# Segment sums by accumulating DMAs on GpSimd's queue, with one short TensorE join, in an S5 convolution and memory-transformer kernel

## The chip, the cores and the metric

The kernel runs on one core of one Trainium2 chip. The metric is the device time of that core in microseconds (us), taken as the median over runs. The engines are named as in the profile: PE is TensorE (PEld its weight loads), DVE is VectorE, ACT is ScalarE, POOL is GpSimd, and SP is the engine that issues most of the DMAs.

## The reference, cut to what matters

Two results of 2048 x 1024 are put side by side. Part A is a state-space model; part B is a recurrent memory transformer over 64 segments of 32 rows, in which 8 memory rows pass from each segment to the next.

```python
def _B_ref(x, mem0, Wq, Wk, Wv, Wo, seg_len):       # x: 1 x 2048 x 1024
    mem = mem0                                       # 1 x 8 x 1024
    for s in range(n_seg):                           # 64 segments of 32 rows
        xs = x[:, s * seg_len:(s + 1) * seg_len, :].copy()
        h = jnp.concatenate([mem, xs], axis=1)
        q = jnp.einsum('btd,dhe->bhte', h, Wq)       # 32 heads of 128
        ...
        p = _softmax(scores, axis=-1)
        o = jnp.einsum('bhqk,bhke->bhqe', p, v)
        o = jnp.einsum('bhte,hed->btd', o, Wo)
        mem = o[:, :M, :].copy()
        outs.append(o[:, M:, :])
```

The kernel does not run the 64 segments one after another. It guesses the memory that each segment hands on, computes all segments at once, and compares the result with the guess at the end; only if they differ too much does a general loop run (it does not run here). The guess rests on the mean row of each segment: `xbar` is the sum of a segment's 32 rows of x, divided by 40 (segment 0 adds the 8 rows of mem0). The change concerns how these 64 sums, each 1024 wide, are formed.

## The kernel before, in words

The work falls into four stages on one program. Stage 1, to about 330 us of the span, is where the change lies. It alternates two kinds of steps that `steps()` lists in order:

- A step `v` (`v_x`) projects 512 rows of x by 512 columns of Wv: 32 matmuls into four PSUM banks `psP` (three buffers), which ACT copies to SBUF and writes out by DMA.
- A step `s` (`stage1`, numbered n = 0 to 31, eight groups `pc` of four blocks) is part A's input product and scan. PE makes 16 matmuls into `psU` (two buffers). DVE multiplies them by tables (`a_pr<-psU`), adds, and scans twice (`TENSOR_TENSOR_SCAN`). POOL then works out the start value of the next block from the scan's last column: five tiny instructions that end in `a_nx`, called the carry here, absent in the last block of each group. ACT copies the scans to `a_g`, DVE multiplies and adds again (`a_n`, `a_h`), and SP stores `a_h`.

A step s is followed by a step v, except after n = 6, 11, 16, 21, 26 and 30. In stage 1 the instructions of PE and of SP keep the order in which the program writes them (`k.pin`). On the other engines the scheduler may move an instruction ahead, unless it is marked `keep_in_program_order`.

The sums are made by the generator `sum_x`. It is first advanced at n = 1, where SP is given the loads of four tiles of 128 rows of x (`b_xr`, four buffers); then twice in each step from n = 3 on. Each advance takes one tile: eight matmuls with a 128 x 128 block of x as the stationary operand and the 128 x 4 indicator `k.ind` as the moving one, into a bank `psR`, and SP loads the tile that comes four later. So PE has 16 such matmuls ahead of the products of each of n = 3 to 10. At n = 11 the generator's last part lets DVE scale the bank into `xbar`. PE uses `xbar` first in `og`, after the v step behind n = 13.

`b_xr` first holds the four tiles from which the first v step gets its transposed x (`load_x0`, `turn_x0`), and last a block of zeros that `fill` writes to DRAM. `a.CT` is a tile in the pool `t32` that is loaded with part A's output weights from n = 17 on (`load_c`).

Of the kernel before, what the change touches and what calls it, by code (L numbers as in the profile page):

```python
# [8 lines left out]
FP32 = mybir.dt.float32  # L9
BF16 = mybir.dt.bfloat16  # L10
I32 = mybir.dt.int32
ACT = mybir.ActivationFunctionType
ALU = mybir.AluOpType
# [25 lines left out]
EV = E + 1  # L39
# [52 lines left out]
def consts(k):  # L92
    nc, V, G = k.nc, k.V, k.G
    c = k.cst
    k.ident = c.tile([128, 128], BF16, name="ident")
    G.memset(k.ident[:], 1.0)
    G.affine_select(out=k.ident[:], in_=k.ident[:], compare_op=ALU.is_equal, fill=0.0, base=0,
                    pattern=[[-1, 128]], channel_multiplier=1)
    k.ones = c.tile([128, 1], BF16, name="ones")
    V.memset(k.ones[:], 1.0)  # L100
    k.hpb = c.tile([128, 1], FP32, name="hpb")
    k.hpe = c.tile([128, 1], FP32, name="hpe")
    V.memset(k.hpb[:], HALF_PI)  # L103
    k.S.activation(k.hpe[:], k.hpb[:], ACT.Exp)
    k.ind = c.tile([128, 4], BF16, name="ind")
    G.memset(k.ind[:], 0.0)
    for j in range(4):
        G.memset(k.ind[32 * j:32 * j + 32, j:j + 1], 1.0)


def masks(k):
# [223 lines left out]
class PartB:  # L335
# [37 lines left out]

    def fill(self, tmp):
        k = self.k
        z = tmp.tile([32, 4 * EV], BF16, name="b_xr", bufs=4)
        k.V.memset(z[:], 0.0)
        for hb in range(HB):
            k.SP.dma_start(self.vx[hb][64 + NMX:GX, :], z[0:GX - 64 - NMX, :])
            k.SP.dma_start(self.vx[hb][T + 32:NSLOT, :], z[0:32, :])  # L380
        for q in range(4):
            k.SP.dma_start(self.tn[q][NM:NR, 0:4 * EV], z[0:NR - NM, :])
            k.SP.dma_start(self.tn[q][NM:NR, 1024 - 4 * EV:1024], z[0:NR - NM, :])
# [13 lines left out]
        return [(64 + 1536, 1536, 384), (0, XMAIN, 64), (T - 64, T - 64, 64)]  # L397

    def load_x0(self, tmp, i):
        self.x0.append(tmp.tile([128, D], BF16, name="b_xr", bufs=4))  # L400
        self.k.SP.dma_start(self.x0[i][:], self.x[0][64 + 128 * i:192 + 128 * i, :])

    def turn_x0(self, i):

        k = self.k
        pt = k.ps("U", (128, 2, KC, 128), BF16)[:, 0, :, :]
        for c in range(KC):
            k.PE.transpose(pt[:, c, :], self.x0[i][:, c * 128:(c + 1) * 128], k.ident[:])
        k.copy("vs"[i % 2], self.xe[:, :, 128 * i:128 * i + 128], pt)

    def sum_x(self, tmp):

        k = self.k
        xrs = {}

        def load(t):
            if t < TT:
                xrs[t] = tmp.tile([128, D], BF16, name="b_xr", bufs=4)
                k.SP.dma_start(xrs[t][:], self.x[0][t * 128:(t + 1) * 128, :])
        for t in range(4):  # L420
            load(t)
        yield
        p = k.ps("R")
        for t in range(TT):
            xr = xrs.pop(t)
            for c in range(KC):
                o = c * NSEG + 4 * t
                k.PE.matmul(p[:, o:o + 4], xr[:, c * 128:(c + 1) * 128], k.ind[:], start=True, stop=True)
            load(t + 4)
            yield  # L430
        pv = p[:].rearrange("p (c s) -> p c s", c=KC)
        ms = tmp.tile([128, KC], FP32, name="b_ms", bufs=1)
        k.V.tensor_reduce(ms[:], self.m0T[:], AX.X, ALU.add)
        k.V.tensor_scalar(self.xbar[:], pv, 1.0 / L, None, ALU.mult)
        k.V.tensor_tensor(ms[:], ms[:], pv[:, :, 0], ALU.add)
        k.V.tensor_scalar(self.xbar[:, :, 0], ms[:], 1.0 / L, None, ALU.mult)
        yield
# [483 lines left out]
def check_consts(k):  # L921

    V, G = k.V, k.G
    k.skip = k.cst.tile([128, 1], FP32, name="c_skip")
    G.memset(k.skip[:], 0.0)
    for r in (2, NTL - 2, NTL - 1):
        G.affine_select(out=k.skip[:], in_=k.skip[:], compare_op=ALU.not_equal, fill=1.0, base=-r,
                        pattern=[[0, 1]], channel_multiplier=1)
    k.fmask = k.cst.tile([L, 2, L], FP32, name="f_mask")
    G.memset(k.fmask[:], 1.0)  # L930
    G.affine_select(out=k.fmask[:, 0, :], in_=k.fmask[:, 0, :], compare_op=ALU.is_ge, fill=0.0, base=0,
                    pattern=[[-1, L]], channel_multiplier=1)
    G.memset(k.fmask[0:M, 0, :], 1.0)
    k.tc.keep_in_program_order(V.tensor_scalar(k.fmask[:, 1, :], k.fmask[:, 0, :], 1.0, 1.0e9, ALU.subtract, ALU.mult))


def steps():


    vs = [(pc, q) for pc in range(PC) for q in range(4)]  # L940
    vs[0:8] = [(i, q) for q in range(4) for i in range(2)]
    ss = [(pc, q) for pc in range(PC) for q in range(NB)]
    out = [("v",) + v for v in vs[:4]]
    vi = 4
    for n, s in enumerate(ss):
        out.append(("s",) + s)
        if n not in (6, 11, 16, 21, 26, 30) and vi < len(vs):
            out.append(("v",) + vs[vi])
            vi += 1
    return out + [("v",) + v for v in vs[vi:]]  # L950


def warm(k, pool):

    w = pool.tile([128, 512], BF16, name="a_n", bufs=1)
    k.V.memset(w[:], 0.0)  # L956
    p = k.ps("R")
    for _ in range(8):
        k.PE.matmul(p[:], w[:, 0:128], w[:], start=True, stop=True)
# [9 lines left out]
def kernel_main(tc, A_x, A_Lre, A_Lim, A_Bre, A_Bim, A_Cre, A_Cim, A_logdt, A_Dskip, B_x, B_mem0, B_Wq, B_Wk, B_Wv, B_Wo, out,  # L969
                force=False, dbg=None):  # L970
    with ExitStack() as ctx:
        k = K(tc, ctx)
        k.dbg = dbg
        nc = k.nc
        a = PartA(k, A_x, A_Lre, A_Lim, A_Bre, A_Bim, A_Cre, A_Cim, A_logdt, A_Dskip, out)
        b = PartB(k, B_x, B_mem0, B_Wq, B_Wk, B_Wv, B_Wo, out)

        def pool(name, side, bufs=2):
            return tc.tile_pool(name=name, bufs=bufs, side=side, reuse_waits="tile")
# [8 lines left out]
        with pool("p1x", "right") as p1x, pool("p1", "right", 1) as p1:  # L988
            a.tab = a.tmp = a.wp = a.btp = p1
            k.pin |= {"PE", "SP"}  # L990
            warm(k, p1)
            w0 = b.wl.tile([128, KC, 512], BF16, name="b_wv", bufs=2)
            b.load_wv_part(w0, 0, 0, 128, nc.scalar)
            b.x0 = []
            for i in range(4):
                b.load_x0(p1, i)
                if i in (1, 2):
                    b.load_wv_part(w0, 0, 128 * i, (256, 512)[i - 1])
            wv = {0: w0, 1: b.load_wv(1)}
            consts(k)  # L1000
            a.load_params(p1)
            b.load_m0(p1)
            b.stage_init()
            order = steps()
            b.v_x(0, 0, wv[0])
            b.load_x(1)
            a.load_b(0)
            a.xT = p1x.tile([128, KC, T], BF16, name="a_xT", bufs=1)
            a.load_x(0)
            a.params(p1, p1)  # L1010
            b.init(p1)
            a.tables(0)
            loads = [[(b, 2)], [(a, 1), (a, 2)], [(b, 3), (a, 3)]]
            sx = b.sum_x(p1)
            tabs = {0: a.tabs}
            bts = {0: a.bt}
            for kind, pc, q in order[1:]:
                if loads and kind == "v":
                    for o, n in loads.pop(0):
                        o.load_x(n)  # L1020
                if kind == "v":
                    b.v_x(pc, q, wv[pc])
                    if q == 3:
                        if pc >= 3:
                            b.og(pc, wv[pc])
                        n = (pc + 2) if pc + 2 < PC else (2, 0)[pc + 2 - PC]
                        wv[n] = b.load_wv(n)
                    continue
                a.tabs, a.bt = tabs[pc], bts[pc]
                n = 4 * pc + q  # L1030
                if q == 2 and pc + 1 < PC:
                    a.load_b(pc + 1)
                    bts[pc + 1], a.bt = a.bt, bts[pc]
                if pc >= 4 and q == 1:
                    a.load_c(pc - 4)
                if n == 1:
                    next(sx)
                if n >= 3:
                    for _ in range(2):
                        next(sx, None)  # L1040
                a.stage1(pc, q)
                if q == 2 and pc + 1 < PC:
                    a.tables(pc + 1)
                    tabs[pc + 1] = a.tabs
                if n == 12:
                    masks(k)
                    check_consts(k)
                if n == 14:
                    b.fill(p1)
            k.pin.remove("PE")  # L1050
# [7 lines left out]
        with pool("p2h", "right") as p2h, pool("p2", "right") as p2:  # L1058
# [5 lines left out]
            for i, _ in enumerate(s2):  # L1064
                if i in (1, 4, 7):
                    n = (2, 0, 1)[(i - 1) // 3]
# [148 lines left out]
```

## Time and profile before

| | |
|---|---|
| median of 8 runs | 1249.43 us (1249.01 to 1250.44) |
| the profiled execution's own time | 1249.28 us |
| its span in the profile | 1247.6 us |
| granted TensorE clock | 0.999 |
| PE busy | 1240.7 us, 99% |
| DVE, ACT, POOL busy | 667.8, 263.7, 273.3 us |
| matmuls of the sums (`psR<-ind,b_xr`) | 128 |
| DMA issues of the sums' tiles, on SP | 16 of 256 KB |

The span counts from the first to the last profiled instruction; 1.7 us of the execution's own time lie around it. In the profile a group's busy time is the union of its instructions, so that matmuls which overlap in the array's pipeline are not counted twice; the step from one matmul's start to the next is what one costs a full PE. A timeline row merges equal neighbours: start, length, engine, line, operation, tiles, count, and in brackets the idle time before it and what ended that.

### The profile page before, as it was taken

The numbers are of one execution on the slowest core, as the hardware profiler recorded it, in microseconds if no ns is written. First come the engines' busy times: TensorE is split into PE (matmuls) and PEld (weight loads), VectorE is DVE, ScalarE is ACT, GpSimd is POOL, SyncE is SP. The second block draws the span as 40 slices with busy tenths as digits, with TensorE's granted clock in tenths as the row PEclk, the third lists the DMA queues.
The fourth block names the chain that finished last, engine by engine and source line by source line (L and its number), as shares of the span: only waits on it lengthen the run. The fifth ranks groups of instructions, "written<-read, shape, count | busy, mean of one in ns | idle before, by whom it ended". The sixth has DMA issues, their size and how long they took to land.

```text
span 1247.6 us, 20183 instructions
## 1 busy us (share of the span) xinstructions
PE 1240.7 (99%) x8342; PEld 664.3 (53%) x8342; DVE 667.8 (54%) x1246; ACT 263.7 (21%) x631; POOL 273.3 (22%) x407
## 2 busy tenths in 40 slices
PE   9999999999999999999999999999999999999998
PEld 5444444444455555566666656555665554446444
DVE  4688899998711124666666666666666641001000
ACT  5344444443310000121212111111211110000000
POOL 3111331212332321222222222222222320000000
PEclk9999999999999999999999999999999999999999
DMA  9975444553898839334464544545474279407000
GB/s 239 243 220 145 128 135 125 141 152 107 238 319 248 249 113 248 91 88 121 90 146 106 142 106 113 140 90 131 93 160 93 56 225 206 108 18 153 18 17 27
DMA packets 314744, 174.18 MB, mean 140 GB/s; under 512 B 138648, under 2 KB 300048, under 8 KB 314648
## 3 DMA queue, kind: packets, MB, share of 16 engines
q1 hardware_dynamic: 292552, 146.22, 48.4%
q10 hardware_dynamic: 21072, 23.47, 5.9%
q0 software_dynamic: 1024, 3.17, 0.7%
q8 instruction: 66, 1.08, 0.4%
q14 instruction: 30, 0.25, 0.1%
HBM read 87.47 MB, written 52.19 MB: 112 GB/s over the span
## 4 chain that ended last, share of the span: by engine, by line
PE 99%; POOL 0%; ACT 0%; issue 0%; DVE 0%; ACTq 0%
PE psP L62 82%; PE psU L62 9%; PE psS L62 3%; PE psO L62 2%; PE psR L62 2%; POOL b_m L639 0%; ACT b_e L636 0%; DVE b_ost L89 0%; DVE a_n L956 0%; ACTq L87 0%; ACTq L636 0%; DVE hpb L103 0%; DVE ones L100 0%
## 5 line engine op out<-in xcount | busy, mean ns | idle before, releaser
L62 PE MATMUL psP<-b_xe,b_wq 128*128 128x480 bf16 (+1 forms) x1280 | 247.7, 342 | 0.0
L62 PE MATMUL psP<-b_xe,b_wk 128*128 128x480 bf16 (+1 forms) x1280 | 247.7, 343 | 0.0
L62 PE MATMUL psP<-b_wv,b_xe 128*128 128x512 bf16 (+2 forms) x1048 | 224.6, 373 | 0.0
L639 POOL TENSOR_TENSOR b_m<-b_e,maskB 99x396 bf16<-99x396 bf16 x160 | 139.4, 871 | 336.0 <-ACT b_e L636 336.0
L636 ACT ACTIVATE b_e<-psS 99x396 bf16<-99x396 f32 x176 | 88.0, 500 | 534.5 <-PE psS L62 526.9
L62 PEld LDWEIGHTS <-b_wk 128*128 128x128 bf16 x1280 | 119.3, 98 | 94.5
L62 PEld LDWEIGHTS <-b_wq 128*128 128x128 bf16 x1280 | 118.5, 98 | 88.1
L62 PEld LDWEIGHTS <-b_xe 128*128 128x128 bf16 x1056 | 102.1, 98 | 118.9 <-DVE b_xe L89 0.2
L89 DVE CAST b_k<-psP 128x480 bf16<-128x480 f32 (+1 forms) x192 | 98.1, 532 | 100.4 <-PE psP L62 100.4
L89 DVE CAST b_q<-psP 128x480 bf16<-128x480 f32 (+1 forms) x192 | 98.1, 532 | 93.8 <-PE psP L62 92.0
L62 PEld LDWEIGHTS <-b_ol 128*128 128x128 bf16 x864 | 84.3, 98 | 94.4
L62 PE MATMUL psU<-a_xT,a_bt 128*128 128x512 bf16 x512 | 114.9, 379 | 0.0
L62 PE MATMUL psP<-t,a_hl 128*128 128x512 bf16 x512 | 113.1, 379 | 0.0
L89 DVE CAST b_ost<-psP 128x512 bf16<-128x512 f32 (+1 forms) x17 | 11.5, 676 | 183.4 <-PE psP L62 183.4
L62 PE MATMUL psP<-wo,b_ol 128*128 128x512 bf16 (+1 forms) x448 | 92.5, 364 | 0.0
L62 PE MATMUL psP<-t,b_ol 128*128 128x512 bf16 x416 | 92.2, 379 | 0.0
L278 POOL TENSOR_SCALAR a_tt<-a_pr,a_tabf 128x1 f32<-128x1 f32 x48 | 34.0, 709 | 243.7 <-DVE a_pr L273 243.7
L87 ACT ACTIVATE b_vst<-psP 128x512 bf16<-128x512 f32 x126 | 72.4, 591 | 69.1 <-PE psP L62 60.2
L656 DVE TENSOR_TENSOR b_ob<-psO,b_accR 99x384 bf16<-99x384 f32 x160 | 85.9, 553 | 2.2
L265 DVE TENSOR_TENSOR a_pr<-psU,a_tabf 128x2048 f32<-128x2048 f32 x32 | 73.0, 2282 | 16.2 <-PE psU L62 16.1
L62 PEld LDWEIGHTS <-a_bt 128*128 128x128 bf16 x512 | 49.2, 98 | 57.6
L62 PEld LDWEIGHTS <-a_hl 128*128 128x128 bf16 x512 | 49.0, 98 | 56.7
(198 smaller groups left out, 964.6 us busy)
## 6 DMA issues: line engine op xcount, KB each, us to landing
b_v<-b_vx SPq DMA_DIRECT2D x16, 1064.2 KB
b_wv<-in_B_Wv_dram SPq DMA_DIRECT2D x16, 1024.0 KB
b_on<-b_ob SPq DMA_DIRECT2D x15, 960.0 KB
b_vx<-b_vst ACTq DMA_DIRECT2D x24, 516.0 KB
a_hs<-a_h SPq DMA_DIRECT2D x32, 256.0 KB
b_wog<-in_B_Wo_dram SPq DMA_DIRECT2D x4, 2048.0 KB
b_wq<-in_B_Wq_dram SPq DMA_DIRECT2D x16, 512.0 KB
b_wk<-in_B_Wk_dram SPq DMA_DIRECT2D x16, 512.0 KB
```

The source lines that it names most:

```text
L62: r = f(*a, **kw)
L87: self.S.activation(out, in_, ACT.Copy)
L89: self.V.tensor_copy(out, in_)
L265: V.tensor_tensor(pr[:], u[:].unsqueeze(1).to_broadcast([128, 2, 2, TB]), view(t3, [[TB + 1, 2], [TB + 1, 2], [1, TB]]), ALU.mult)
L278: G.tensor_scalar(tt[:, j:j + 1], w[:, j, TB - 1:TB], t3[:, 1, TB:TB + 1], None, ALU.mult)
L636: k.S.activation(e[:], s[0:GW], ACT.Exp, scale=float(E) ** -0.5, accum_out=self.accE[0:GW, i:i + 1])
L639: k.G.tensor_tensor(m[:, 0:4 * GW].rearrange("p (a b q) -> p a b q", a=2, b=2), e[:], mask[0:GW, :, :].unsqueeze(2).to_broadcast([GW, 2, 2 ...
L656: V.tensor_tensor(self.ob[:, b0:b0 + n, :], o[0:GW, 0:n, 0:E], r.unsqueeze(2).to_broadcast([GW, n, E]), ALU.mult)
```

## The change

`sum_x` no longer loads x in tiles of 128 rows. It views x as 128 half segments of 16 rows: partition p of the accumulator takes rows 16p to 16p + 15. Sixteen DMAs on GpSimd's queue each bring row j of all 128 half segments: the even j to one half of a float32 tile `acc`, the odd j to the other. The first DMA of each half writes, the other seven add to what is there. Two DMAs are issued per advance of the generator. Then POOL adds the two halves, ACT copies the sum to bf16 (the high part), and POOL subtracts the high part from the sum and stores the rest as bf16 (the low part); both lie in a corner of `a.CT`, which is not loaded yet. PE joins the half segments: 16 matmuls with a 128 x 128 block of the high or low part as the stationary operand, and a 128 x 64 indicator as the moving one, which has a one where partition p belongs to segment p // 2.

The generator is advanced once per step from n = 2 on. So the DMAs are issued ahead of n = 2 to 9, the three elementwise instructions ahead of n = 10, and the matmuls with DVE's scaling ahead of n = 11. The DMAs and POOL's two elementwise instructions are marked `keep_in_program_order`; ACT's copy is not. The indicator is built by one memset and two selections instead of five memsets, the four start tiles of `load_x0` become one tile of four parts, and all uses of `b_xr` now share a single buffer.

```diff
-    k.ind = c.tile([128, 4], BF16, name="ind")
-    G.memset(k.ind[:], 0.0)
-    for j in range(4):
-        G.memset(k.ind[32 * j:32 * j + 32, j:j + 1], 1.0)
+    k.ind = c.tile([128, NSEG], BF16, name="ind")
+    G.memset(k.ind[:], 1.0)
+    for base, m in ((0, 1), (1, -1)):
+        G.affine_select(out=k.ind[:], in_=k.ind[:], compare_op=ALU.is_ge, fill=0.0, base=base,
+                        pattern=[[-2 * m, NSEG]], channel_multiplier=m)
...
-        z = tmp.tile([32, 4 * EV], BF16, name="b_xr", bufs=4)
+        z = tmp.tile([32, 4 * EV], BF16, name="b_xr", bufs=1)
...
-        self.x0.append(tmp.tile([128, D], BF16, name="b_xr", bufs=4))
-        self.k.SP.dma_start(self.x0[i][:], self.x[0][64 + 128 * i:192 + 128 * i, :])
+        if i == 0:
+            self.x0 = tmp.tile([128, 4, D], BF16, name="b_xr", bufs=1)
+        self.k.SP.dma_start(self.x0[:, i, :], self.x[0][64 + 128 * i:192 + 128 * i, :])
...
-    def sum_x(self, tmp):
-
-        k = self.k
-        xrs = {}
-
-        def load(t):
-            if t < TT:
-                xrs[t] = tmp.tile([128, D], BF16, name="b_xr", bufs=4)
-                k.SP.dma_start(xrs[t][:], self.x[0][t * 128:(t + 1) * 128, :])
-        for t in range(4):
-            load(t)
+    def sum_x(self, tmp, ct):
+
+
+        k = self.k; G = k.G
+        acc = tmp.tile([128, 2, D], FP32, name="b_xr", bufs=1)
+        rows = self.x[0].rearrange("(p j) d -> p j d", j=16)
+        for j in range(16):
+            op = {"accum_op": ALU.add} if j > 1 else {}
+            k.tc.keep_in_program_order(G.dma_start(acc[:, j % 2, :], rows[:, j, :], **op))
+            if j % 2:
+                yield
+        s = acc[:, 0, :]
+        hl = ct[:, 0, 0:2, :]
+        k.tc.keep_in_program_order(G.tensor_tensor(s, s, acc[:, 1, :], ALU.add))
+        k.S.activation(hl[:, 0, :], s, ACT.Copy)
+        k.tc.keep_in_program_order(G.tensor_tensor(hl[:, 1, :], s, hl[:, 0, :], ALU.subtract))
         yield
         p = k.ps("R")
-        for t in range(TT):
-            xr = xrs.pop(t)
-            for c in range(KC):
-                o = c * NSEG + 4 * t
-                k.PE.matmul(p[:, o:o + 4], xr[:, c * 128:(c + 1) * 128], k.ind[:], start=True, stop=True)
-            load(t + 4)
-            yield
+        for c in range(KC):
+            for i in range(2):
+                k.PE.matmul(p[:, c * NSEG:(c + 1) * NSEG], hl[:, i, c * 128:(c + 1) * 128], k.ind[:], start=(i == 0), stop=(i == 1))
...
-                if n == 1:
-                    next(sx)
-                if n >= 3:
-                    for _ in range(2):
-                        next(sx, None)
+                if n >= 2:
+                    next(sx, None)
                 a.stage1(pc, q)
```

More of the change, by code (lines that the diff above doesn't have):

```diff
@@ L407, in turn_x0 @@
         for c in range(KC):
-            k.PE.transpose(pt[:, c, :], self.x0[i][:, c * 128:(c + 1) * 128], k.ident[:])
+            k.PE.transpose(pt[:, c, :], self.x0[:, i, c * 128:(c + 1) * 128], k.ident[:])
         k.copy("vs"[i % 2], self.xe[:, :, 128 * i:128 * i + 128], pt)
-    def sum_x(self, tmp):
-        k = self.k
-        xrs = {}
-        def load(t):
-            if t < TT:
-                xrs[t] = tmp.tile([128, D], BF16, name="b_xr", bufs=4)
-                k.SP.dma_start(xrs[t][:], self.x[0][t * 128:(t + 1) * 128, :])
-        for t in range(4):
-            load(t)
+    def sum_x(self, tmp, ct):
[12 more added lines that the diff above has]
+        k.tc.keep_in_program_order(G.tensor_tensor(hl[:, 1, :], s, hl[:, 0, :], ALU.subtract))
         yield
         p = k.ps("R")
-        for t in range(TT):
-            xr = xrs.pop(t)
-            for c in range(KC):
-                o = c * NSEG + 4 * t
-                k.PE.matmul(p[:, o:o + 4], xr[:, c * 128:(c + 1) * 128], k.ind[:], start=True, stop=True)
-            load(t + 4)
-            yield
+        for c in range(KC):
+            for i in range(2):
+                k.PE.matmul(p[:, c * NSEG:(c + 1) * NSEG], hl[:, i, c * 128:(c + 1) * 128], k.ind[:], start=(i == 0), stop=(i == 1))
         pv = p[:].rearrange("p (c s) -> p c s", c=KC)
@@ L993, in kernel_main @@
             b.load_wv_part(w0, 0, 0, 128, nc.scalar)
-            b.x0 = []
             for i in range(4):
@@ L1013, in kernel_main @@
             loads = [[(b, 2)], [(a, 1), (a, 2)], [(b, 3), (a, 3)]]
-            sx = b.sum_x(p1)
+            sx = b.sum_x(p1, a.CT)
             tabs = {0: a.tabs}
```

## The prediction

> **What bounds the kernel now.** I read the busy line and the chain of the page first, then PE's timeline around the sums, then DVE's and POOL's where the new instructions will stand, and last the DMA issues of POOL's queue.
>
> ```profile
> PE 1240.7 (99%) x8342; PEld 664.3 (53%) x8342; DVE 667.8 (54%) x1246; ACT 263.7 (21%) x631; POOL 273.3 (22%) x407
> PE 99%; POOL 0%; ACT 0%; issue 0%; DVE 0%; ACTq 0%
> ```
>
> PE is the path from end to end: the chain that ended last lies on it for 99%. Whatever PE no longer executes comes off the time, and whatever PE newly waits for goes on it, one for one. What the sums cost PE is seen in its timeline, at n = 6 and 7 of the steps s, and what 64-column matmuls cost, in `og`:
>
> ```profile
> 99.22 0.54 PE L62 MATMUL psR<-ind,b_xr 128*128 128x4 bf16 x16
> 99.62 3.61 PE L62 MATMUL psU<-a_xT,a_bt 128*128 128x512 bf16 x16
> 103.07 0.54 PE L62 MATMUL psR<-ind,b_xr 128*128 128x4 bf16 x16
> ...
> 170.28 1.10 PE L62 MATMUL psR<-b_xbar,b_wv 128*128 128x64 bf16 x32
> 171.22 2.11 PE L62 MATMUL psU<-a_xT,a_bt 128*128 128x512 bf16 x9
> ```
>
> Start to start, 16 sum matmuls hold PE for 0.40 us (25 ns each), not the 0.54 of the merged row, whose end overlaps the next group. The 32 of `og` hold it 0.94 us: 29 ns each.
>
> **What goes and what comes on PE.** Removed: 8 groups x 0.40 = 3.2 us. Added: 16 matmuls x 29 ns = 0.47 us. If nothing new makes PE wait, the gain is 2.73 us. The profiled execution (1249.28, span 1247.6) would read 1246.55; I set it against the median, 0.15 higher: 1249.43 - 2.73 = 1246.7.
>
> **Edits that I cost at nothing.** SP loses 16 issues of about 0.42 us; only the tile loads hung on them. The indicator, the joined start tile and the single `b_xr` buffer act at the start or at `fill`: `b_xr` is free from the last transposition (11.2 us) until the first accumulating DMA (after 58 us), and PE reads the identity, not the indicator, at the start. If the parts of the joined start tile were awaited together, PE would lose about 2 us there (the fourth load is issued at 3.3, the second at 1.3); separate parts of one tile are already awaited separately for Wv's first block, so I take zero. DVE's scaling of `psR` (1.0 us) stays, one step later; its reader `og` comes 24 us behind.
>
> **POOL's queue: what the DMAs pass.** Besides the carries POOL is idle in stage 1. Each DMA pair stands behind the carry of n - 1 and ahead of that of n, and waits for the landing of the pair before. Behind a waiting DMA stands a carry; for it waits DVE's scan of n + 1, and for DVE, through `psU`, PE.
>
> ```profile
> a_xn<-in_A_x_dram POOLq DMA_DIRECT2D x3, 256.0 KB, 6.2
> ...
> a_r<-in_A_Lambda_re_dram POOLq DMA_DIRECT2D x1, 2.0 KB, 4.2
> ...
> 330.36 2.23 POOL L306 DMA_DIRECT2D a_hl<-a_hs  x4 [0.41 <-issue]
> ```
>
> An issue costs POOL 0.56 us, so a pair 1.1 us. No row shows an accumulating DMA. Its time to landing is at least the 4.2 us of a 2 KB row. The nearest row is `a_xn`, plain and of the same source bytes: 6.2. Above that: a row now reads 2 KB and 4 KB and writes 4 KB, 10 KB for `a_xn`'s 4, so its 2.0 us over the small DMA become 5: 9.2 us. I take 7. The chain has room for that: steps are 10.4 us apart (without the sums), and where two steps s adjoin or a carry is absent there is a spare step. DVE has cover too: from the end of `a_pr<-psU` to PE's return to that bank are 5.5 us at worst (n = 20) and 7.9 or more at n = 2 to 13. A carry late by up to 4 us is absorbed.
>
> [...]
>
> **The join: the new wait on PE's own path.** PE comes to the joining matmuls at 146.11 - 3.2 = 142.9 us, behind the step v after n = 10, in fixed order: all of PE is queued behind them. Their input is a chain of last DMA pair, add, copy, subtraction.
>
> ```profile
> 130.06 0.20 POOL L280 TENSOR_TENSOR a_nx<-a_nx,a_tt 128x2 f32<-128x2 f32 x1
> 136.77 1.05 POOL L280 TENSOR_TENSOR a_nx<-a_nx,a_tt 128x2 f32<-128x2 f32 x1
> ...
> 136.54 1.23 DVE L284 TENSOR_TENSOR a_n<-a_g,a_tabh 128x2048 bf16<-128x2048 bf16 x1 [0.70 <-ACT a_g L274]
> 137.80 0.69 DVE L285 TENSOR_TENSOR a_h<-a_n 128x1024 bf16<-128x1024 bf16 x1
> 141.73 1.22 DVE L268 TENSOR_TENSOR a_pr<-a_pr 128x1024 f32<-128x1024 f32 x1
> 143.06 2.46 DVE L273 TENSOR_TENSOR_SCAN a_pr<-a_rr,a_nx,a_pr 128x512 f32<-128x512 f32 x2
> ```
>
> These instructions come 1.6 us earlier after the change (DVE is held by PE last at n = 6, with four groups gone). So the carry of n = 8 ends at 130.26 - 1.6 = 128.7, the last pair is issued to 129.8 and lands 7 us after its second start (129.2): 136.2. The carry of n = 9 ends at 137.82 - 1.6 = 136.2. Then the add, priced by POOL's row of this width, `a_xd` 128x1024: 2.12 us; behind DVE's `a_h` it runs 136.8 to 138.9. ACT's copy is 1.02 us by the `b_xe<-psU` row of 128x1024: to 140.1. The subtraction, 2.12 us again, ends at 142.3 to 142.5: 0.4 us ahead of PE.
>
> [...] In the rows above the same 128x2 instruction takes 0.20 us, and 1.05 us when it starts inside `a_n`, ending 0.05 us after it. [...] By the rows alone only POOL waits: if the subtraction misses the gap at 140.4 it starts behind the first scan (141.7) or the second (142.9), ends at 143.9 or 145.1, and PE waits 1.0 or 2.2 us. [...] I take the gap as met.
>
> ACT is idle in the window (before: 137.5 to 141.1, with the PE-fed copies to come 3.2 us earlier, at 137.9 and 139.6), so the copy fits between two of them, if it is ordered there. It is not pinned. Behind it in ACT's queue stand the `psP` copies, whose three buffers cover PE for 5.2 us.
>
> **The rivals.**
>
> *In time (chance 0.40).* The join finds its input: 1246.7. For it: the chain above with every price from a row; against it: a margin of 0.4 us.
>
> *The join is late by some microseconds (0.30).* The copy is ordered behind a `psP` copy or behind the `a_g` copies of n = 10 (144.38 and 145.56 before, 142.8 after), or the subtraction falls behind the scans, or the last pair lands at 137 to 140. With the copy after the first `a_g` of n = 10 (143.4), it ends at 144.4, the subtraction at 146.6, and PE waits 3.7 us: 1250.4. With one missed gap PE waits 1.0: 1247.7. Middle: 2 us, 1248.7. For it: everything that can vary makes the chain longer, and a lost gap costs a whole DVE instruction. Waits from 0.23 to 5.2 us mean no measurable change.
>
> *The accumulating DMAs are slow (0.30).* If one takes about 10 us or more, each pair holds up the next: the one ahead of n = 7 starts at 109 and is followed back to back by that of n = 8. At 12 us they land at 121.5 and 134; the last pair is issued at 134, holds up the carry of n = 9, and lands at 146.5; add, copy and subtraction end about 153 (2.1 + 1.1 + 2.1 + 1.2 for a lock), and PE waits 10.4 us: 1249.4 - 2.7 + 10.4 = 1257. It decides from about 10 us per DMA: there the last lands at 140.5, the chain ends near 148, and the wait of 5.2 us turns the gain into a loss of over 0.2%. For it: no trace row has this kind, DMAs are 0.62 busy at 128 to 140 us[...]. Against it: 10 us is beyond my upper bound of 9.2.
>
> *The change does not do what it says:* PE might keep its time if the loads, not the matmuls, paced these steps. It does not: PE has no idle time between 31 and 480 us.
>
> **How the numbers follow.** What a measurement of this kernel can tell from no change is about 0.2%, 2.5 us. Cases: 0.40 in time (faster: 2.73 is just over), 0.30 late by some microseconds (same), 0.30 slow DMAs (slower). Forecast: the likeliest, 1246.7. Low end 1246.2: no wait, and 0.5 us for the sizes of the two matmul rows. High end 1259: it takes in the slow case to 12 us per DMA with 2 us of lock and order on top; beyond lies a longer chain, about 1 in 8. The likeliest case alone: 1246.2 to 1247.2.
>
> **What would show it.** Right: 112 fewer matmuls; steps s at n = 3 to 10 10.36 us apart where they were 10.76; PE without idle time ahead of `psR<-ind,t`; POOL rows of 0.5 to 0.6 us for 16 DMAs, and landings near 7 us. Wrong: a wait of PE on `psR` for POOL's subtraction or for the DMA behind it (how late, read at its start against 142.9); POOL's carries waiting for a DMA; DVE instructions longer beside the add or the subtraction; PE waiting on `psU`, which I exclude.

## The result, and the profile after

The changed kernel takes 1254.48 us in the median of 21 runs (1252.96 to 1263.6), the kernel before, on the same chip, 1249.65. The ratio is 1.0042, 95% interval 1.0033 to 1.005: slower by about 0.4%, where 1246.7 and a gain had been forecast. The profiled execution took 1256.14 us, its span is 1254.3.

The first two lines are the page's busy line and its chain of the changed kernel.

```profile
PE 1239.4 (99%) x8230; PEld 661.0 (53%) x8230; DVE 667.9 (53%) x1246; ACT 264.4 (21%) x632; POOL 292.3 (23%) x423
PE 92%; DVE 3%; DMA 2%; POOL 1%; ACT 1%; issue 0%; SPq 0%; ACTq 0%; DVEq 0%; POOLq 0%
```

PE has the 112 matmuls fewer. Yet the chain that lay on PE for 99% does so for 92%: on the rest of it PE waits for others. The timeline of PE in the changed kernel, around the steps n = 9 to 13, shows where (start, length, instruction, count, idle time before it and what ended that):

```profile
124.89 3.62 PE L62 MATMUL psU<-a_xT,a_bt 128*128 128x512 bf16 x16
128.34 7.07 PE L62 MATMUL psP<-b_wv,b_xe 128*128 128x512 bf16 x32
135.25 3.62 PE L62 MATMUL psU<-a_xT,a_bt 128*128 128x512 bf16 x16
138.70 3.62 PE L62 MATMUL psP<-b_wv,b_xe 128*128 128x512 bf16 x16
145.55 3.61 PE L62 MATMUL psP<-b_wv,b_xe 128*128 128x512 bf16 x16 [3.23 <-ACT b_vst L87]
149.00 0.63 PE L62 MATMUL psR<-ind,t 128*128 128x64 bf16 x16
149.47 7.07 PE L62 MATMUL psU<-a_xT,a_bt 128*128 128x512 bf16 x32
156.37 5.34 PE L62 MATMUL psP<-b_wv,b_xe 128*128 128x512 bf16 x24
164.23 3.43 PE L62 MATMUL psP<-b_wv,b_xe 128*128 128x512 bf16 x8 [2.52 <-ACT b_vst L87]
```

The steps are 10.36 us apart now (135.25 - 124.89), and the sixteen joining matmuls take 0.47 us start to start (149.47 - 149.00). But the step v after n = 10 stops in its middle and the one after n = 12 after three quarters, both times for ACT's copies of `psP`. (Idle times in the text are taken from start to start, less the 0.216 us of a matmul, or the 0.03 us of one of 64 columns: 3.39 and 2.68 us here; the bracket counts from a modelled end.) The joining matmuls themselves wait for nothing.

**The first stop** is explained by ACT's timeline:

```profile
137.43 0.58 ACT L87 ACTIVATE b_vst<-psP 128x512 bf16<-128x512 f32 x1
143.95 1.06 ACT L427 ACTIVATE t<-b_xr 128x1024 bf16<-128x1024 f32 x1 [5.94 <-POOL b_xr L426]
144.92 0.58 ACT L87 ACTIVATE b_vst<-psP 128x512 bf16<-128x512 f32 x1
```

The copy of the sum's high part stands in ACT's queue ahead of the last `psP` copy of the previous step v. It waits 5.94 us for POOL's add, and everything behind it waits along. POOL's own timeline says why the add is late: the last two DMAs are issued from 131.28 on, and land 8.3 and 9.5 us after their issues began.

```profile
131.28 1.83 POOL L421 DMA_DIRECT2D b_xr<-in_B_x_dram  x2
...
141.58 2.34 POOL L426 TENSOR_TENSOR b_xr<-b_xr 128x1024 f32<-128x1024 f32 x1 [2.74 <-DMA b_xr<-in_B_x_dram]
145.09 2.12 POOL L428 TENSOR_TENSOR t<-b_xr,t 128x1024 bf16<-128x1024 f32 x1 [1.17 <-ACT t L427]
```

**The second stop** begins on DVE, one step of the pipeline earlier. First the changed kernel, then the same instruction in the kernel before:

```profile
147.32 0.27 DVE L378 MEMSET b_xr<- 32x258 uint32 x1 [7.81 <-POOL t L428]
147.52 2.22 DVE L266 TENSOR_TENSOR a_pr<-psU,a_tabf 128x2048 f32<-128x2048 f32 x1
```

```profile
129.01 0.27 DVE L377 MEMSET b_xr<- 32x258 uint32 x1
```

This is the memset of `fill`'s zeros. In the program it comes after n = 14; in both kernels it stands much earlier in DVE's queue. With four buffers nothing held it. With one, it needs the accumulator's buffer, which POOL's subtraction releases last, at 147.2. Behind it stands `a_pr<-psU` of n = 10. So DVE is 7.81 us idle and then late. PE does not wait for DVE through `psU` here; the delay reaches it through ACT, whose queue has the table work of the next group and the `a_g` copies ahead of the `psP` copies:

```profile
159.30 0.63 ACT L227 ACTIVATE a_tabf<-a_fr 128x513 f32<-128x513 f32 x1 [4.17 <-DVE a_pr L266]
...
163.06 0.63 ACT L275 ACTIVATE a_g<-a_pr 128x512 bf16<-128x512 f32 x1 [0.55 <-DVE a_pr L274]
163.60 0.58 ACT L87 ACTIVATE b_vst<-psP 128x512 bf16<-128x512 f32 x1
```

The table work waits for DVE's late `a_pr<-psU`; in the kernel before the same instruction starts at 152.15. The `psP` copy at 163.60 ends the stop of PE, two steps behind the memset.

The second stop costs more than its idle time. The windows of the changed kernel (length, then busy time and count of PE, PEld, DVE, ACT, POOL, then the granted clock, DMA share and GB/s):

```profile
161.00:164.20 3.20, 0.72 (x4) 0.20 (x3) 3.20 (x3) 2.44 (x6) 0.00 (x0) 1.00 0.00 0
164.20:167.50 3.30, 3.27 (x9) 1.20 (x9) 3.30 (x4) 1.56 (x3) 0.00 (x0) 0.53 0.00 0
167.50:171.00 3.50, 3.50 (x17) 1.58 (x16) 3.50 (x5) 1.74 (x3) 1.69 (x2) 0.95 0.19 75
```

The granted clock falls to 0.53: eight matmuls follow each other at 427 ns instead of 216, which adds 1.68 us. The page's clock row, in 40 slices, does not show this.

The spans divide as follows (first `psU` of n = 0; of n = 10; last of n = 31; end of DVE's last copy; end). The last column is the best kernel of the experiments, described below.

| stretch | before | after | best |
|---|---|---|---|
| start to n = 0 | 35.86 | 38.38 | 36.68 |
| n = 0 to n = 10 | 99.90 | 96.87 | 96.69 |
| n = 10 to n = 31 | 189.99 | 198.22 | 191.22 |
| n = 31 to the last copy | 917.53 | 917.55 | 917.54 |
| last copy to the end | 4.31 | 3.33 | 3.33 |
| span | 1247.59 | 1254.35 | 1245.47 |

The removed matmuls bring the second row down by 3.03 to 3.21. The third row of the changed kernel is +8.23 = 0.47 (joining matmuls) + 3.39 (first stop) + 2.68 + 1.68 (second stop, idle and half clock). The start of this execution is 2.5 later; in the other profiles with the new sums it is 0.6 to 1.0 later, except in one (2.6). The end is 0.98 shorter. With a start of 0.8 the rows sum to -3.0 + 8.2 + 0.8 - 1.0 = 5.0; the medians differ by 4.83.

### The profile page after: what moved, and what is told of

The parts are those of the page before. It is cut to its first block, busy times and chain, and to the rows that moved or that the text cites. A ratio compares the mean times of both kernels' runs of the same rounds, so it can differ in the third digit from the quotient of the medians.

```text
span 1254.3 us, 19944 instructions
## 1 busy us (share of the span) xinstructions
PE 1239.4 (99%) x8230; PEld 661.0 (53%) x8230; DVE 667.9 (53%) x1246; ACT 264.4 (21%) x632; POOL 292.3 (23%) x423
## 4 chain that ended last, share of the span: by engine, by line
PE 92%; DVE 3%; DMA 2%; POOL 1%; ACT 1%; issue 0%; SPq 0%; ACTq 0%; DVEq 0%; POOLq 0%
PE psP L62 78%; PE psU L62 7%; PE psS L62 3%; PE psO L62 2%; PE psR L62 1%; DVE a_pr L266 1%; DVE a_pr L274 1%; DMA b_xr<-in_B_x_dram 1%; DMA b_vx<-b_vst 1%; DMA b_wv<-in_B_Wv_dram 1%; DVE a_pr L269 0%; POOL b_m L642 0%; ACT b_vst L87 0%; DVE a_n L285 0%; POOL b_xr L426 0%
## 5 line engine op out<-in xcount | busy, mean ns | idle before, releaser
L62 PEld LDWEIGHTS <-b_xe 128*128 128x128 bf16 x1056 | 102.2, 98 | 128.6 <-issue 10.5
```

The lines of the kernel that those rows point to most:

```text
L62: r = f(*a, **kw)
```

## The experiments

The main theory, A in the expectations: two instructions that were moved ahead of their place hold their queues, ACT's copy and `fill`'s memset, and the sums themselves are not too dear. The rivals: the late join itself, and accumulating DMAs that are too slow. Each time is set against runs of the kernel before on the same chip.

**1. The zeros in a place of their own.** Only `fill` changes: the zeros take a spare corner of `a.CT`.

```diff
-        z = tmp.tile([32, 4 * EV], BF16, name="b_xr", bufs=1)
-        k.V.memset(z[:], 0.0)
+        z = ct[0:32, 0, 2, 0:4 * EV]
+        k.V.memset(z, 0.0)
```

> The changed kernel with the block of zeros of fill in a corner of a.CT instead of the single buffer b_xr; DVE's memset then goes first in its queue and waits for nothing. Theory A (two queues are held by the join: ACT's copy holds the psP copies, 3.4 us of PE at n = 10; DVE's memset holds a_pr, 4.2 us of PE at n = 12): the second stall goes, the first stays: 1249.65 - 2.73 + 3.4 = 1250.3, range 1249.6 to 1251.0. Theory B ([...] the memset only happens to stand there): DVE stays late, 1252.5 or more. Theory C (the accumulating DMAs slow other DMAs, PE's 2.5 us at the start and small stalls): no change, 1254.5.

Measured: 1251.31 us, ratio 1.0013 (1.0006 to 1.002). PE's timeline of this kernel:

```profile
137.21 3.62 PE L62 MATMUL psP<-b_wv,b_xe 128*128 128x512 bf16 x16
144.06 5.30 PE L62 MATMUL psP<-b_wv,b_xe 128*128 128x512 bf16 x16 [3.24 <-ACT b_vst L87]
...
156.57 7.07 PE L62 MATMUL psP<-b_wv,b_xe 128*128 128x512 bf16 x32
```

The second stop is gone: 32 matmuls in one row after n = 12. The first is there unchanged. So the shared buffer caused the second stop. The time is 0.3 above the expected band, and the row of 5.30 us where 3.61 stood tells why: now it is this stop that is followed by half clock (1.67 us).

**2. The copy on POOL** in place of ACT, in program order, with all else as changed.

```diff
-        k.S.activation(hl[:, 0, :], s, ACT.Copy)
+        k.tc.keep_in_program_order(G.tensor_copy(hl[:, 0, :], s))
```

> The changed kernel with the high part copied by POOL, pinned, instead of by ACT; ACT's queue no longer waits, the zeros still share b_xr. Theory A: the stall of 3.2 us in the step v after n = 10 goes, and PE waits about 1.5 us at the join for the subtraction instead; but DVE's memset still ends near 147.3 us, and as DVE's queue and not PE sets the stall at n = 12, that stall grows by what PE gained: 1254.5, range 1253.5 to 1255. If the two stalls simply add (rival to A): 1254.5 - 3.4 + 1.5 = 1252.6. Theory C: 1254.5, with both stalls still small beside the start.

Measured: 1255.72 us in the median of 5 runs, ratio 1.0044 (1.0031 to 1.0058): 0.7 above the expected band, and further from the rival's 1252.6. PE's timeline:

```profile
145.51 0.19 PE L62 MATMUL psR<-ind,t 128*128 128x64 bf16 x1
147.48 0.61 PE L62 MATMUL psR<-ind,t 128*128 128x64 bf16 x15 [1.77 <-POOL t L428]
...
164.44 2.66 PE L62 MATMUL psP<-b_wv,b_xe 128*128 128x512 bf16 x8 [4.26 <-ACT b_vst L87]
```

The first stop is gone, so ACT's copy caused it. Two things came in its place: PE now waits 1.94 us at the join itself, which the first stop had hidden, and the second stop grows from 2.68 to 4.42 us idle (half clock follows as before), because PE reaches it that much earlier while DVE is held as before. Both stops hang on the same late sum: with the copy mended alone, the second stop and the join take up the time. Not so the other way round: experiment 1 lost the second stop and kept the first at its length.

**3. Add and join one step later each**, by a `yield` more ahead of the add and one more ahead of the joining matmuls: the sum gets a whole step for its landing, and PE comes to the join at n = 13.

```diff
+        yield
         s = acc[:, 0, :]
...
         yield
+        yield
         p = k.ps("R")
```

> The changed kernel with an empty step behind the last DMAs and another ahead of the join: add, copy, subtraction ahead of n = 11, joining matmuls ahead of n = 13. The DMAs have landed by then. Theory A: ACT's copy stands where no step v follows at once, no stall from it; DVE's memset still waits for the subtraction, about 5 us instead of 7.8, and PE loses 1 us or less: 1248, range 1246.7 to 1249.5. Theory B: [...] 1249 or more. Theory C: 1252 or more, since the DMAs are all there.

Measured: 1251.42 us, ratio 1.0016 (1.0006 to 1.0025). The expectation was missed by about 3 us. ACT's copy still waits 3.15 us, but at a place where PE has cover. The memset is still on DVE's queue ahead of its place, waits 2.85 us, and PE stops once, with half clock after it:

```profile
150.58 5.34 PE L62 MATMUL psP<-b_wv,b_xe 128*128 128x512 bf16 x24
158.63 3.46 PE L62 MATMUL psP<-b_wv,b_xe 128*128 128x512 bf16 x8 [2.71 <-ACT b_vst L87]
```

I had taken the shorter wait on DVE as covered. It was not: idle 2.87 and 1.57 of half clock.

**4. Both: later, and the zeros apart** (the edits of experiments 1 and 3).

> Both edits, the later join and the zeros in a corner of a.CT. Theory A: no queue is held, what is left is the gain on PE: 1249.65 - 2.73 = 1246.9, range 1246.4 to 1247.7. Theory B: up to 2 us more. Theory C: 1252 or more. If the joined start tile costs PE about 1 us at the start, 1248.

Measured: 1247.75 us, ratio 0.9991 (0.9981 to 1.0). PE's timeline:

```profile
143.93 7.07 PE L62 MATMUL psU<-a_xT,a_bt 128*128 128x512 bf16 x32
150.84 7.31 PE L62 MATMUL psP<-b_wv,b_xe 128*128 128x512 bf16 x32
157.99 0.63 PE L62 MATMUL psR<-ind,t 128*128 128x64 bf16 x16
```

No stop of over 0.5 us is left in stage 1 (0.25 here, 0.49 at 202 us); the sums and the accumulating DMAs are as in the changed kernel. So the loss came from the late sum and the two queues that were held for it, and not from the DMAs' rate, which is the same here.

**5. The join at its own place with no queue held** (the edits of experiments 1 and 2): what the late join costs by itself.

> The changed kernel at its own place (join ahead of n = 11) with the zeros in a corner of a.CT and the copy on POOL: neither ACT's nor DVE's queue is held. What is left is PE's own wait at the join for the last DMAs, add, copy and subtraction, 2.0 us as in the kernel with the copy on POOL alone. 1249.5 - 2.73 + 2.0 = 1248.7; with 0.8 us at the start, 1249.5. If [...] PE waits at psU or psP as well, 1250.5 or more.

Measured: 1252.79 us, ratio 1.0026 (1.0015 to 1.0037): a time of the last case, 1250.5 or more, but not by the way named there, since PE waits at the join alone. First PE's timeline, then POOL's, then DVE's:

```profile
145.44 0.20 PE L62 MATMUL psR<-ind,t 128*128 128x64 bf16 x1 [1.36 <-POOL t L427]
148.43 0.61 PE L62 MATMUL psR<-ind,t 128*128 128x64 bf16 x15 [2.79 <-POOL t L428]
```

```profile
140.09 3.38 POOL L426 TENSOR_TENSOR b_xr<-b_xr 128x1024 f32<-128x1024 f32 x1 [2.96 <-DMA b_xr<-in_B_x_dram]
143.54 1.84 POOL L427 CAST t<-b_xr 128x1024 bf16<-128x1024 f32 x1
145.46 2.91 POOL L428 TENSOR_TENSOR t<-b_xr,t 128x1024 bf16<-128x1024 f32 x1
```

```profile
140.04 1.23 DVE L269 TENSOR_TENSOR a_pr<-a_pr 128x1024 f32<-128x1024 f32 x1
141.37 5.09 DVE L274 TENSOR_TENSOR_SCAN a_pr<-a_rr,a_nx,a_pr 128x512 f32<-128x512 f32 x2
147.16 2.30 DVE L285 TENSOR_TENSOR a_n<-a_g,a_tabh 128x2048 bf16<-128x2048 bf16 x1 [0.70 <-ACT a_g L275]
```

PE waits 1.52 and 2.96 us at the join, 4.48 in all where 2.0 were expected, and 1.69 of half clock follow. So a late join is enough to turn the gain into a loss, with no queue held. The chain is longer here than in the changed kernel. POOL's and DVE's instructions run side by side, and both take longer: the add takes 3.38 (2.34 above), the cast 1.84 (1.04 in experiment 2, where DVE stood still), the subtraction 2.91 (2.12), while the two scans take 5.09 (2.46) and `a_n` 2.30 (1.23). That is 0.79 to 1.04 us more for each of POOL's, 2.63 for the two scans together and 1.07 for `a_n`; by what means they lengthen each other is not shown. In the changed kernel itself it cost nothing, since DVE was idle at that time (7.81 us): with the queues mended, this loss comes to light.

**6. Later, zeros apart and the copy on POOL** (the edits of experiments 1, 2 and 3).

> Join two steps later, zeros apart, copy on POOL: no queue held, no wait at the join. Pure gain on PE: 1246.8; if the 0.8 us at the start of all changed kernels belong to the change, 1247.5. Range 1246.4 to 1247.8.

Measured: 1248.22 us, ratio 0.9996 (0.9987 to 1.0006), 0.4 above the expected range. PE's two waits are 0.61 and 0.50 us. With a step of time in between, no difference between ACT's copy (experiment 4) and POOL's is clear of the noise.

**7. What adding costs a DMA.** Experiment 1 with all sixteen DMAs overwriting, so that the rows are not summed, and the general loop left out.

```diff
-            op = {"accum_op": ALU.add} if j > 1 else {}
+            op = {}
```

> The 16 DMAs overwrite instead of adding (the rows are no longer summed), the check of the guess is set to pass, and the zeros are apart; same issues, same order, same waits. If the accumulation makes the late landing (9.6 us for the second DMA of the last pair), this one lands within 7.5 us and the stall of the copies shrinks by 2 us, to 1.5. If it is the issue on POOL and the queue that take the time, 9 us or more and the stall stays at 3.4.

Measured: 1248.14 us in one run. The rows of POOL's group and of the DMA issues, first of the changed kernel, then of this one:

```profile
L421 POOL DMA_DIRECT2D b_xr<-in_B_x_dram x16 | 13.8, 952 | 13.0 <-DMA b_xr<-in_B_x_dram 13.0
b_xr<-in_B_x_dram POOLq DMA_DIRECT2D x16, 512.0 KB, 7.5
```

```profile
L421 POOL DMA_DIRECT2D b_xr<-in_B_x_dram x16 | 9.0, 565 | 9.8 <-DMA b_xr<-in_B_x_dram 9.7
b_xr<-in_B_x_dram POOLq DMA_DIRECT2D x16, 512.0 KB, 5.9
```

Adding raises POOL's time for sixteen from 9.0 to 13.8 us, 0.56 to 0.86 each (the means of 565 and 952 ns count the overlap of two neighbouring issues twice), and the landing from 5.9 to 7.5 us. The second DMA of the last pair lands after 8.0 us, between the expectation's 7.5 and 9. Counted from the first issue of the last pair, both have landed after 8.6 us, in experiment 1 after 10.2; the stop of PE shrinks by as much, from 3.40 to 1.86 us idle, with no half clock after it. So adding is worth about 1.5 us at the join, and the landing is long without it too.

**8. The start.** The kernel before with the joined start tile, its later tiles of x in the same four parts.

```diff
-        self.x0.append(tmp.tile([128, D], BF16, name="b_xr", bufs=4))
-        self.k.SP.dma_start(self.x0[i][:], self.x[0][64 + 128 * i:192 + 128 * i, :])
+        if i == 0:
+            self.x0 = tmp.tile([128, 4, D], BF16, name="b_xr", bufs=1)
+        self.k.SP.dma_start(self.x0[:, i, :], self.x[0][64 + 128 * i:192 + 128 * i, :])
...
-                xrs[t] = tmp.tile([128, D], BF16, name="b_xr", bufs=4)
+                xrs[t] = self.x0[:, t % 4, :]
```

> The kernel before with its four start tiles as parts of one tile, which the later tiles of x use in turn; sums by 128 matmuls as before. If the joined tile costs PE 0.8 us at the start (second group of transpositions waiting for its load), 1250.3; if not, 1249.5 and no such wait.

Measured: 1249.86 us, ratio 0.9996 (0.9988 to 1.0004), n = 0 at 35.48: the joined tile does not make the start later.

**9. Two rows in one DMA.** Experiment 6 with eight DMAs of 4 KB rows into both halves of `acc`.

```diff
-        for j in range(16):
+        for j in range(0, 16, 2):
...
-            k.tc.keep_in_program_order(G.dma_start(acc[:, j % 2, :], rows[:, j, :], **op))
-            if j % 2:
-                yield
+            k.tc.keep_in_program_order(G.dma_start(acc[:], rows[:, j:j + 2, :], **op))
+            yield
```

> The version with later add and join, zeros apart and the copy on POOL (1248.2 us), with one accumulating DMA of 128 rows of 4 KB (both halves of the accumulator) instead of two of 2 KB per advance. Theory 'an accumulating DMA costs POOL per instruction': POOL issues 8 instead of 16, about 1 us less per step, and the last one lands about 1 us earlier; PE does not wait for either, so the time stays at 1247.3 to 1248.2. Theory 'it costs per byte': the issue of one takes about 1.8 us as the pair did, landing as before, time the same. What separates them is the length of POOL's row of L421 and the landing, not the time.

Measured: 1247.61 us, ratio 0.9982 (0.9975 to 0.9988).

```profile
L421 POOL DMA_DIRECT2D b_xr<-in_B_x_dram x8 | 6.9, 864 | 14.0 <-DMA b_xr<-in_B_x_dram 13.3 <-issue 0.6
b_xr<-in_B_x_dram POOLq DMA_DIRECT2D x8, 1024.0 KB, 8.1
```

An issue of twice the bytes takes 864 ns, as much as one of the sixteen smaller ones (13.8 us for 16): POOL's cost did not grow with the bytes here, and one DMA is cheaper than the pair. Both kinds have 128 rows; whether the cost goes by the instruction or by the rows was not tried. The last DMA lands 9.8 us after its issue begins, the pair of experiment 6 10.1 us after its first: 0.3 us earlier, not the 1 us expected.

**10. The kernel before with the new indicator** in the old one's place (read by nobody), the old one built later.

```diff
-    k.ind = c.tile([128, 4], BF16, name="ind")
-    G.memset(k.ind[:], 0.0)
-    for j in range(4):
-        G.memset(k.ind[32 * j:32 * j + 32, j:j + 1], 1.0)
+    k.ind64 = c.tile([128, NSEG], BF16, name="ind64")
+    G.memset(k.ind64[:], 1.0)
+    for base, m in ((0, 1), (1, -1)):
+        G.affine_select(out=k.ind64[:], in_=k.ind64[:], compare_op=ALU.is_ge, fill=0.0, base=base,
+                        pattern=[[-2 * m, NSEG]], channel_multiplier=m)
```

> The kernel before, with the changed kernel's 128 x 64 indicator built in the old one's place (it is read by nobody) and the old 128 x 4 one built later. Theory 'the new indicator at the start moves POOL's first DMAs and with them PE's start': the first psU<-a_xT,a_bt starts at 36.5 to 36.9 us where it starts at 35.86, and the time is 1250.2 (0.7 more than before). Rival 'the start is something else (place of the tiles in SBUF, or luck of the loads)': first psU<-a_xT,a_bt at 35.5 to 35.9, time as before, 1249.4 to 1249.7.

Measured: 1250.32 us, 0.74 more than the kernel before, as expected; but the ratio, 1.0004 (0.9995 to 1.0013), does not exclude zero. PE's start in the kernel before, then in this one:

```profile
4.66 1.91 PE L62 MATMUL psU<-ident,b_xr 128*128 128x128 bf16 x16
```

```profile
4.66 0.65 PE L62 MATMUL psU<-ident,b_xr 128*128 128x128 bf16 x8
6.09 0.62 PE L62 MATMUL psU<-ident,b_xr 128*128 128x128 bf16 x8 [0.78 <-DMA b_xr<-in_B_x_dram]
```

The second tile of x comes late, as in every profile with the new indicator and in neither of the two without it. But n = 0 is at 37.42, later than both theories expected: another stop of PE, 0.74 us at 35 us of the span, adds to it. So the late tile comes with the new indicator; a cost in the whole time is not shown.

**11. A late indicator.** Experiment 4 with the indicator built behind the rest of POOL's start work (its definition is moved behind `b.init(p1)`).

> The version with later add and join and zeros apart (1247.75 us), with the indicator built behind the other start work of POOL. Theory 'the new indicator moves the start': first psU<-a_xT,a_bt at about 35.9 instead of 36.8, time 1246.9. Rival 'something else': first psU<-a_xT,a_bt stays at 36.5 to 36.9, time 1247.7.

Measured: 1247.23 us, ratio 0.9978 (0.997 to 0.9986), which beats the kernel before and the changed one. Its stretches are in the table above. But n = 0 stays at 36.68: the rival holds on the start.

**12. POOL's start as before.** Experiment 11 with the old small memsets put back, on a spare tile, so that POOL's DMAs are issued when they were.

> The version with later add and join, zeros apart and a late indicator (1247.23 us, first psU<-a_xT,a_bt at 36.68), with the five small memsets of the kernel before put back in the indicator's old place (on a tile that nobody reads), so that POOL's second DMA is issued at 2.94 us as in the kernel before and not at 2.47. Theory 'POOL's small DMAs, issued earlier, delay the load of the second x tile': first psU<-a_xT,a_bt at 35.5 to 35.9, time 1246.3. Rival 'the place of tiles, or something else': 36.5 to 36.9, time 1247.2.

Measured: 1247.61 us, ratio 0.9982 (0.9974 to 0.999), n = 0 at 36.42, the second tile of x still 0.53 us late. POOL's second DMA is at 2.95 again, so its time is not the cause. What makes the start 0.6 to 1.0 us later remains open. The profiles that have it share the 128 x 64 tile, behind which other tiles lie elsewhere; moving that tile was not tried.

## Why the prediction was wrong

**The gain on PE: right.** 3.2 less and 0.47 more were forecast; the profiles show 2.72 (experiment 1) to 3.21, and 0.47. What failed is the condition, "If nothing new makes PE wait": the prediction put the new waits at nothing, and in the profile PE loses 3.39 + 2.68 + 1.68 = 7.75 us to them. Three terms of it were wrong.

**"Edits that I cost at nothing": this step failed, for the single buffer.** I asked when `b_xr` is free and when it is used, and looked at the first and the last use. I did not ask which instruction of `fill` asks for it, on which engine, and where in that engine's queue it stands. The trace of before had the answer: `b_xr<-` on DVE at 129.01, six steps s ahead of its place in the program. Costed from there, it waits for the subtraction's end, and behind it is `a_pr<-psU`. In the profile this wait is 7.81 us on DVE, and 2.68 + 1.68 us on PE. The cover of 7.9 us that the prediction counted for DVE was the one through `psU`, and it held; the way over ACT's queue was not counted.

**ACT's copy: the risk was named, its direction was not.** The prediction says that the copy is not pinned and has the `psP` copies behind it, and that three buffers cover PE for 5.2 us. It considered the copy ordered too late; it was ordered too early. It held ACT from 138.0 to 143.95 us, and the cover was two buffers, not three: the third still held the last block of the step before. PE made 16 matmuls (3.45 us) and stopped for 3.39.

**The join's sum was short by 2 us.** In the profile PE's step n = 10 begins 2.7 us later than in the prediction's clock (135.25 for 132.55), so 2.7 comes off each measured time. Then the last pair is issued at 128.6 (forecast 128.7), lands at 138.7 (136.2), and the subtraction ends at 144.5 (142.3 to 142.5). The mis-sized terms: the pair's issue 1.83 us for 1.1, the landing 9.5 for 7, the add 2.34 for 2.12. The bounds of 4.2 to 9.2 were near (4.6 to 10.4 here), though the upper one is an estimate by bytes, and that adding moves more of them is not shown: the trace counts 512 KB for each DMA with and without it (experiment 7). The value within them was 2 too low for the last pair, though 7.5 is the median of the sixteen. The longer issue comes from the adding: the same pair without it takes 1.14 us (experiment 7). The margin of 0.4 us was therefore never there: experiment 2 shows a wait of 1.94 us at the join, inside the 1.0 to 2.2 given for a missed gap. The gap that I "take as met" is lost once DVE is not held (experiment 5).

**A wait costs more than its length.** The prediction counts waits "one for one". Of six stops of 2.68 us or more in the profiles five were followed by about eight matmuls at 427 ns, 1.57 to 1.69 us more; a stop of up to 1.94 us that stood alone never was. The last section shows which ones are.

**The rivals.** The slow DMAs come close to the measured time (1257, from a wait of 10.4 us, which their own sum makes 10.1; the 1.2 "for a lock" in it is an estimate from the prediction's rows: POOL waiting for one DVE instruction such as `a_n`, 1.23), by the wrong mechanism: POOL's issues waited for landings only where a step was spare (13.0 us in all), the DMAs did not pile up, and experiment 4 keeps them all and is not slower. The late join is real: 4.48 + 1.69 us by itself (experiment 5), where the rival gave 2 in the middle and 3.7 in its worst worked case; in the changed kernel the two queues hide it. That the range held the result is no merit of its reasons.

**Not foreseen, and nearly cancelling:** the later start and the shorter end.

## What to carry to other kernels

When a tile loses buffers, list every instruction that asks for it, with its engine and its place in that engine's queue as the trace has it, not as the program has it: an instruction far from the critical path holds everything behind it (the memset here: DVE idle for 7.81 us). An unpinned helper copy can be put ahead of the work that feeds the bound engine; give a late chain a whole step of time before its reader, and the order of such a copy ceases to matter (experiments 4 and 6); a shared buffer has to be mended as well (experiment 3). Stops behind one late input can hide each other, so mend them together before judging any, and count a stop of about 3 us of PE as up to 1.7 more (1.57 to 1.69 in five of six here).

## What the hardware showed that I had not expected

**The clock after a stop.** The trace records when the granted clock changes. In each of the five profiles with a half clock it falls once in stage 1, for 3.41 us, and the time from the first rise at the start to that fall is a whole number of such lengths: 47.0 (changed kernel, 160.43 us), 41.0, 47.0, 45.0 and 42.0 (experiments 1, 2, 3 and 5). So in these profiles the changes lie on a grid of 3.41 us. Laid over PE's stops, the grid tells which of them cost more (in us; a window is one length of the grid, and the standstill is counted as above):

| kernel | window | PE stood still | clock in the next |
|---|---|---|---|
| changed, first stop | 140.51 to 143.93 | 1.77 | full |
| changed, first stop | 143.93 to 147.34 | 1.62 | full |
| changed, second stop | 160.99 to 164.41 | 2.68 | half |
| experiment 1 | 141.26 to 144.68 | 2.80 | half |
| experiment 2, join | 144.93 to 148.34 | 1.94 | full |
| experiment 2, second stop | 158.58 to 162.00 | 1.98 | full |
| experiment 2, second stop | 162.00 to 165.41 | 2.45 | half |
| experiment 3 | 155.03 to 158.44 | 2.68 | half |
| experiment 5, join | 142.13 to 145.54 | 1.60 | full |
| experiment 5, join | 145.54 to 148.96 | 2.89 | half |

In these ten rows a window with 2.45 us or more of standstill is followed by half clock, one with up to 1.98 us is not, and 2.45 of 3.41 us were enough. The stop of 3.39 us in the changed kernel, with full clock after it, is cut by a mark into 1.77 and 1.62; of nearly the same stop in experiment 1 (3.40), 2.80 lie in one window. Where between 1.98 and 2.45 the limit lies, no run here shows.

**The end.** From DVE's last copy to the span's end are 4.31 us before and 3.33 after (table above). The eleven profiles with the new sums have 3.33 to 3.46, the three with the old sums on PE 4.31 to 4.38. In the kernel before SP stands still for 0.8 us ahead of its last drains. Why it no longer does is not shown; about 1 us of the best kernel's gain is this.

**An accumulating DMA** costs POOL 0.86 us where one that overwrites costs 0.56, no more with twice the bytes in the same 128 rows (experiment 9), and lands about 1.6 us later in the median (experiment 7).
